# Filter MLP and FFN passage of a Hyena filter kernel: positions loaded in two halves, loads held back, and the first tile's sums put ahead of two units' spectra

## The chip, the cores and the metric

One core of one Trainium2 chip. Its engines are TensorE (PE: matrix products into PSUM), VectorE (DVE), ScalarE (ACT), GpSimd (POOL) and SyncE (SP, which only issues transfers). Each works through its own instructions in order; a semaphore holds an instruction until what it needs is done. Transfers (DMAs) are issued from the queues of SP, ACT and POOL and share 16 DMA engines. The metric is the device time of one execution in microseconds (us); lower is better.

## The reference

```python
h_filt = (np.maximum(pos_emb @ w1, 0.0) @ w2) * np.exp(-0.01 * np.arange(S))[:, None]
u = x * v                                   # x, v: (4, 12544, 128) float32
Uf = np.fft.rfft(u, n=2 * S, axis=1)
Hf = np.fft.rfft(h_filt, n=2 * S, axis=0)   # pos_emb: (12544, 64), w1: (64, 64), w2: (64, 128)
y = np.fft.irfft(Uf * Hf[None], n=2 * S, axis=1)[:, :S]
t = (x * y).reshape(50176, 128)
h = np.maximum(np.maximum(t @ moe_w1, t @ moe_w2), t @ moe_w3)   # 128 -> 768, moe weights float64
out = h @ moe_w_out                                              # 768 -> 128
```

A filter is made by a small MLP over position embeddings and damped by a window; the input is convolved with it along the sequence, gated by x, and sent through a maxout feed-forward network (FFN).

## The kernel before, in words

The long transform is split by hand into two steps: sums over 98 (or 82, for the filter) blocks of 128 positions give N1 = 90 values of an index k1, then a second step works per k1. Everything is float32. The schedule is manual: every engine executes in the order in which the Python code issues, and tile pools with a fixed number of buffers decide when a buffer may be written again.

1. **Prologue, to about 117 us.** PE runs products on a zero tile (`warm_up`, 4 records each). POOL issues the loads of the window, of an identity (`eye`), of a permutation (`back`) and of `w1`; SP and ACT issue eight loads of the position embeddings `pos` (64 rows at a time, 5.0 to 5.5 KB per row). `window_back` transposes the window on PE, lets ACT copy it into `winT`, multiplies by `back` and copies the result to `winr`. The filter MLP then has eight steps. `mlp_in(i)` is 32 matmuls (64 records and as many weight loads) into one of two PSUM tiles `pm`; it takes positions 127 - 16 i downward of each block, so steps 0 to 3 need columns 64 to 127 and steps 4 to 7 the rest. `mlp_out(i)` is two VectorE operations that apply ReLU and the window and write into `hs`. Between them VectorE multiplies the first two *units* of batch 0 (`u_mul`; a unit is 4 channels' worth of x and v, loaded by `u_load` in two DMAs of 196 KB with 392-byte pieces), and `turn2` transposes them on PE. Then come 16 *quads* of the filter (`quad`: 16 matmuls, one ACT copy) and 16 pairs of units, each two quads and a `turn2`. Beside them VectorE converts the FFN's float64 weights piece by piece (`some`, 12 operations for each of 8 jobs) from `raw` tiles; the first two raw loads are issued by SP in the prologue, the others by POOL.
2. **Second step of filter and batch 0, to about 303 us.** Per pair of k1: products, butterflies, the product with the filter's spectrum, and the way back; results go to DRAM (`zd`). At its end the first units of batch 1 are transposed for the next stage.
3. **Passage.** With the first FFN tile, `t_load` fetches the tile's z values (two DMAs) and x (four). `t_sums` forms sums and differences of the two z halves on VectorE, `t_last` multiplies them on PE by the inverse table `f4p` and VectorE multiplies the result by x into `gt`. Units 2 and 3 of batch 1 are treated here too: `u_products` does a unit's 16 matmuls (32 records) and an ACT copy `high` and returns a function that does its two VectorE operations (line 426), which write the *spectrum*; `u_first` is both at once.
4. **FFN with the convolutions of batches 1 to 3 beside it, to the end.** `up` makes a piece of the hidden layer (two products, an ACT ReLU and a VectorE maximum), `down` the product with `moe_w_out`; steps of the next batch's convolution are laid out by slot beside them (units 4 and 5 of batch 1 at slots 0 and 2). The last batch runs with fewer products.

Banks: `u_products` takes turns over two PSUM banks (`cps`), so unit 4 reuses the bank of unit 2 and unit 5 that of unit 3; `up` and the first `t_last` take turns over three (`hps`). Two buffers serve `high`, two serve `raw`.

Of the kernel before, what the change touches and what calls it, by code (L numbers as in the profile page):

```python
# [10 lines left out]
FP32 = mybir.dt.float32  # L11
# [5 lines left out]
P = 128  # L17
# [10 lines left out]
HH = NH // 2  # L28
# [63 lines left out]
def kernel(  # L92
# [15 lines left out]
    nc = tc.nc  # L108
    NG, _, _, B, NB = x.shape
    FO, S = posT.shape  # L110
# [18 lines left out]
    f1_d = nc.inline_tensor(f1_t, name="f1_const").ap()  # L129
    f1h_d = nc.inline_tensor(f1h_t, name="f1h_const").ap()  # L130
# [64 lines left out]
    def scratch(name, bufs):  # L195
        return sml.tile([P, 2 * HF], I32, tag=name, name=name, bufs=bufs)[:]

    def load_raw(i, h, eng):
        r = scratch("raw", 2)
        if i < 3:  # L200
            src = (moe_w1, moe_w2, moe_w3)[i].bitcast(I32).rearrange("(g c) f -> c g f", c=GC)
            for c in range(GC):
                eng.dma_start(r[c * NG:(c + 1) * NG],
                                  src[c][:, h * 2 * HF:(h + 1) * 2 * HF])
        else:
            src = moe_w_out.bitcast(I32).rearrange("(c p) d -> p c d", p=P)
            eng.dma_start(r.rearrange("p (c d) -> p c d", c=NF // 2),
                              src[:, h * NF // 2:(h + 1) * NF // 2, :])
        return r
# [52 lines left out]

    specH = pin.tile([P, N1, 2, FO], FP32, name="specH")
    pos = specH[:].rearrange("p k r f -> p (k r f)")[:, 0:HH * P]
    posv = pos.rearrange("f (n p) -> f p n", p=P)
    hs = spec[0:64 + HH].rearrange("p k r d -> p (k r d)")[:, 0:FO * P].rearrange(
        "n (f r t) -> n f r t", r=2, t=64)
# [2 lines left out]
    w2x = pin.tile([P, D], FP32, name="w2x")  # L270
    win = sml.tile([64 + HH, P], FP32, name="win")
    winT = sml.tile([P, 2, 64 + HH], FP32, name="winT")
    winr = sml.tile([64 + HH, 2, 64], FP32, name="winr")
    back = sml.tile([P, 2, 64], FP32, name="back")
    f1h = sml.tile([64 + HH, 2, 2 * N1], FP32, name="f1h")
    warm = sml.tile([P, 256], FP32, name="warm")
# [9 lines left out]
    nc.gpsimd.dma_start(eye[:], eye_d)  # L286
    nc.gpsimd.dma_start(back[:].rearrange("p r t -> p (r t)"), back_d)
    for h in range(2):
        nc.gpsimd.dma_start(w1_sb[64 * h:64 * h + 64], w1[:, :])
    cuts = (0, 11, 21, 31, HH)  # L290
    for j, (lo_, hi_) in enumerate(zip(cuts, cuts[1:])):
        for h in range(2):
            (nc.scalar if (h + j) % 2 else nc.sync).dma_start(
                pos[64 * h:64 * h + 64, lo_ * P:hi_ * P],
                posT[:, (h * HH + lo_) * P:(h * HH + hi_) * P])
    for r in range(2):
        nc.scalar.copy(winT[:, r, 0:64], warm[:, 0:64])

    def warm_up(n):

        ps = fps.tile([P, 1024], FP32, tag="cv", name="pw")
        for _ in range(n):
            halves_mm(ps[:, 0:256], warm[:, 0:P], warm[:], True, True)

    def window_back():
        pw = fps.tile([P, 1024], FP32, tag="cv", name="pw")
        nc.tensor.transpose(pw[:, 0:64 + HH], win[:], eye[0:64 + HH, 0:64 + HH])
        for r in range(2):
            for h in range(2):
                c = 64 * (h ^ r)  # L310
                nc.scalar.copy(winT[:, r, c:c + HH], pw[:, 64 * h:64 * h + HH])
        for r in range(2):
            nc.tensor.matmul(pw[0:64 + HH, 512 + 64 * r:576 + 64 * r], winT[:, r], back[:, r],
                             start=(r == 0), stop=True, skip_group_check=True)
        nc.scalar.copy(winr[:].rearrange("n r t -> n (r t)"), pw[0:64 + HH, 512:512 + P])

    def w2_order():
        nc.scalar.copy(w2x[:].rearrange("f (c g) -> f c g", c=GC),
                       w2_in[:].rearrange("f (g c) -> f c g", c=GC))

    def mlp_in(i):

        ps = pms[i % 2]
        for q in range(8):
            for r in range(2):
                for h in range(2):
                    c = 64 * (h ^ r)
                    nc.tensor.matmul(  # L328
                        ps[c:c + HH, 512 * r + q * FO:512 * r + (q + 1) * FO],
                        posv[64 * h:64 * h + 64, P - 1 - 2 * (8 * i + q) - r, :],  # L330
                        w1_sb[64 * h:64 * h + 64], start=(q == 0), stop=True,
                        skip_group_check=True)
    def mlp_out(i):
        v = pms[i % 2][0:64 + HH].rearrange("n (r t f) -> n r f t", r=2, t=8)
        for r in range(2):
            nc.vector.scalar_tensor_tensor(
                out=hs[:, :, r, 8 * i:8 * i + 8], in0=v[:, r], scalar=0.0,
                in1=winr[:, r, None, 8 * i:8 * i + 8].to_broadcast([64 + HH, FO, 8]),
                op0=ALU.max, op1=ALU.mult)
# [9 lines left out]
    def u_load(b, u):  # L349
        c, g0 = divmod(u, NG // 4)  # L350
        ts = []
        for src in (xr, vr):
            t = pools(b, u).tile([P, 4, NB], FP32, tag=f"u{len(ts)}", name="ut")
            nc.sync.dma_start(
                t[:], src[4 * g0:4 * g0 + 4, :, c, b, :].rearrange("g p n -> p g n"))
            ts.append(t)
        us[u] = ts

    def u_mul(u):
        a, v = us[u]  # L360
        nc.vector.tensor_tensor(out=a[:], in0=a[:], in1=v[:], op=ALU.mult)  # L361
# [68 lines left out]
    def u_first(*args):  # L430
        u_products(*args)()
# [269 lines left out]
    def t_sums(i, eng=nc.gpsimd, parts=(0, 1)):  # L701
        z0, z1 = zts[i]
        if 0 in parts:
            evens_[i] = hp.tile([N1, 512], FP32, tag="even", name="even", bufs=2)
        even = evens_[i]
        for a, (out, op) in enumerate(((even[:], ALU.add), (z1, ALU.subtract))):
            if a not in parts:
                continue
            if i[0] == 0 or i[1] < NT // 2:
                eng.tensor_tensor(out=out, in0=z0, in1=z1, op=op)  # L710
            else:
                nc.vector.scalar_tensor_tensor(out=out, in0=z1, scalar=sign_t[:, 0:1], in1=z0,
                                               op0=ALU.mult, op1=op)
        if 1 in parts:
            zts[i] = evens_.pop(i)[:], z1
# [145 lines left out]
    raws, todo = [], []  # L861
# [15 lines left out]
    def turn2(u):  # L877

        t = utp.tile([NB, 8, 2, 64], FP32, tag="uT", name="uT")
        ps = fps.tile([P, 1024], FP32, tag="cv", name="pst")  # L880
        for v in range(2):
            turn(u + v, ps[:, 512 * v:512 * v + 512])
        nc.scalar.copy(t[:], ps[0:NB, :].rearrange("n (s t r) -> n s r t", s=8, r=2))
        uts[u] = t
# [2 lines left out]
        ps = fps.tile([P, 1024], FP32, tag="cv", name="ps1")  # L887
        first_halves(ps, lhs, table, dst, nc.scalar.copy)

    warm_up(22)  # L890
    window_back()
    warm_up(3)
    nc.scalar.dma_start(f1h[:], f1h_d)
    nc.scalar.dma_start(w2_in[0:FO], w2[:, :])
    nc.scalar.dma_start(w2_in[FO:P], w2[:, :])
    nc.scalar.dma_start(f1q[:], f1_d)
    raws.append(load_raw(*jobs[0], nc.sync))
    u_load(0, 0)
    u_load(0, 1)
    raws.append(load_raw(*jobs[1], nc.sync))  # L900
    for u in range(2, 6):
        u_load(0, u)
    for i in range(9):
        if i < 8:
            mlp_in(i)
        if i:
            mlp_out(i - 1)
        if i in (4, 5):
            u_mul(i - 4)
        if i == 7:  # L910
            turn2(0)
    w2_order()
    mps.close()
    fps = fin.enter_context(tc.tile_pool(name="fps", bufs=4, space=PSUM))
# [217 lines left out]
    for n, (b, i) in enumerate(tiles[:LAST]):  # L1132
        if i == 0:
            plan, pairs_from = plans[b]
        if n == 0:
            t_load(*tiles[0])
            t_load(*tiles[1])
            u_first(2)
            third = u_products(3)
            t_sums(tiles[0], nc.vector)  # L1140
            t_last(tiles[0], next(hbanks))
            third()
        for f in range(NF):

            if i < NT - 2:
                if f == 0:
                    t_load(*tiles[n + 2])
            elif i == NT - 1 and f < 2 and n + 1 + f < len(tiles):
                t_load(*tiles[n + 1 + f])
            turn_ = i == NT - 1  # L1150
            if f == 4 and n + 1 == LAST:
                t_sums(tiles[n + 2], nc.vector)
            h = up((b, i), f)
            for a in range(2):
                if f == plan[i][a]:
                    t_sums(tiles[n + 1],
                           nc.vector if turn_ or i * NF > pairs_from else nc.gpsimd, (a,))
            late.append(((b, i), f, h))
            if len(late) > 2:
                down(*late.pop(0))  # L1160
            if f == plan[i][2]:
                t_last(tiles[n + 1])
            if f == 5 and n + 1 == LAST:
                t_last(tiles[n + 2])
            run(besides.pop(n * NF + f, ()))
# [28 lines left out]
    for i in range(0, NT, 2):  # L1194
        h = {}
# [67 lines left out]
```

## Time and profile before

| What | us |
|---|---|
| median of 3 runs | 2282.13 |
| lowest and highest | 2281.03, 2283.14 |
| profiled execution | 2286.24 |
| its span, first to last instruction | 2284.5 |
| PE busy | 2256.9 |
| DVE busy | 1561.3 |
| ACT busy | 1174.9 |
| POOL busy | 878.6 |

The profile is of one execution; positions in time are given from the start of its span. In its rows, "PE" is the matrix product and "PEld" the weight load that runs beside it; a row gives the line of the kernel, the engine, the operation, what it writes and reads, and behind an arrow what the engine last waited for. The chain of waits follows the work back from the last instruction to whatever released each step; "issue" in it is time in which the engine waited for nothing that the profile shows. Line 328 is `mlp_in`, 336 `mlp_out`, 165 a quad, 413 a unit's products in the later batches, 710 `t_sums`, 731 the product with x, and 156 a helper that all products in halves go through.

### The profile page before, as it was taken

The numbers are of one execution on the slowest core, as the hardware profiler recorded it, in microseconds if no ns is written. First come the engines' busy times: TensorE is split into PE (matmuls) and PEld (weight loads), VectorE is DVE, ScalarE is ACT, GpSimd is POOL, SyncE is SP. The second block draws the span as 40 slices with busy tenths as digits, with TensorE's granted clock in tenths as the row PEclk, the third lists the DMA queues.
The fourth block names the chain that finished last, engine by engine and source line by source line (L and its number), as shares of the span: only waits on it lengthen the run. The fifth ranks groups of instructions, "written<-read, shape, count | busy, mean of one in ns | idle before, by whom it ended". The sixth has DMA issues, their size and how long they took to land.

```text
span 2284.5 us, 68468 instructions
## 1 busy us (share of the span) xinstructions
PE 2256.9 (99%) x27855; PEld 1377.3 (60%) x27855; DVE 1561.3 (68%) x2854; ACT 1174.9 (51%) x2125; POOL 878.6 (38%) x1087
## 2 busy tenths in 40 slices
PE   8999999999999999999999999999999999999998
PEld 7989866655555556655555556655555556666665
DVE  5579867668787757657878756767878854544443
ACT  2688844456666534456666534456666622222222
POOL 2045434323333333423333334423333326666666
PEclk9999999999999999999999999999999999999999
DMA  8778989799999689879999889779999732222221
GB/s 182 188 220 278 303 178 182 141 217 245 238 220 245 181 171 174 164 186 250 238 234 239 206 162 186 160 174 254 234 241 238 199 86 56 56 68 64 62 56 22
DMA packets 473269, 411.03 MB, mean 180 GB/s; under 512 B 327865, under 2 KB 374426, under 8 KB 472954
## 3 DMA queue, kind: packets, MB, share of 16 engines
q1 hardware_dynamic: 445954, 329.48, 63.9%
q0 software_dynamic: 26288, 75.47, 11.0%
q8 instruction: 219, 3.59, 0.7%
q10 hardware_dynamic: 712, 1.70, 0.3%
q14 instruction: 96, 0.79, 0.1%
HBM read 262.84 MB, written 84.67 MB: 152 GB/s over the span
## 4 chain that ended last, share of the span: by engine, by line
PE 96%; DMA 1%; DVE 1%; issue 1%; ACT 0%; POOL 0%; SPq 0%; POOLq 0%; DVEq 0%; ACTq 0%
PE hps L156 44%; PE ops L156 19%; PE ops L804 6%; PE cps L413 5%; PE cps L156 4%; PE ps L156 3%; PE cps L474 3%; PE ps L165 3%; PE cps L484 3%; PE sps L1010 2%; PE gps L992 2%; PE last L156 1%; PE pst L366 1%; PE pm L328 1%; DMA back<-back_const 0%
## 5 line engine op out<-in xcount | busy, mean ns | idle before, releaser
L156 PE MATMUL hps<-gt,w_sb 128*64 128x392 f32 x6144 | 1150.7, 494 | 0.7 <-DVE gt L731 0.7
L741 ACT ACTIVATE hid<-hps 128x392 f32<-128x392 f32 x768 | 383.8, 500 | 703.3 <-PE hps L156 686.8
L156 PEld LDWEIGHTS hps<-gt,w_sb 128*64 128x64 f32 x6144 | 430.7, 137 | 422.0 <-issue 385.8
L744 DVE TENSOR_TENSOR hid<-hid,hps 128x392 f32<-128x392 f32 x768 | 428.3, 558 | 334.0 <-PE hps L156 325.6
L156 PE MATMUL ops<-hid,wo_sb 128*64 128x392 f32 x2304 | 480.0, 492 | 0.0
L526 POOL TENSOR_TENSOR cb<-cb,xs 128x512 f32<-128x512 f32 x135 | 174.1, 1290 | 462.6 <-DVE xs L523 345.8
L156 PEld LDWEIGHTS ops<-hid,wo_sb 128*64 128x64 f32 x2304 | 171.8, 137 | 207.4 <-issue 199.4
L426 DVE TENSOR_TENSOR spec<-cps,high 128x360 f32<-128x360 f32 x188 | 140.9, 790 | 127.2 <-ACT high L422 127.2
L499 DVE TENSOR_TENSOR cb<-cps,eo 128x512 f32<-128x512 f32 (+1 forms) x288 | 175.3, 650 | 74.0 <-ACT eo L496 74.0
L759 POOL DMA_DIRECT2D out_dram<-ot x96 | 75.4, 785 | 343.9 <-ACT ot L757 296.5
L514 ACT ACTIVATE xs<-cb 32x512 f32<-32x512 f32 x270 | 169.5, 628 | 20.5 <-DVE cb L499 11.5
L515 ACT COPY xs<-cb 32x512 f32<-32x512 f32 x270 | 166.3, 616 | 3.2
L422 ACT COPY high<-cps 128x360 f32<-128x360 f32 x94 | 75.0, 798 | 179.7 <-PE cps L413 145.9
L413 PEld LDWEIGHTS cps<-f1q,uT 98*64 98x64 f32 x3008 | 131.2, 138 | 29.3 <-issue 23.7
L530 DVE TENSOR_TENSOR xs<-cb 128x256 f32<-128x256 f32 x270 | 140.9, 567 | 9.2 <-POOL cb L526 9.0
L413 PE MATMUL cps<-f1q,uT 98*64 98x90 f32 x3008 | 135.5, 242 | 1.9 <-DVE uT L397 1.5
L382 POOL COPY planes<-ut 128x784 uint16<-128x784 uint16 x90 | 76.3, 848 | 155.0 <-DVE ut L361 141.3
L507 POOL DMA_DIRECT2D zd<-cb x135 | 92.8, 687 | 64.5 <-DVE cb L499 56.9
L156 PEld LDWEIGHTS cps<-f4p,even 90*64 90x64 f32 x1552 | 89.5, 138 | 35.0 <-issue 32.6
L828 POOL DMA_DIRECT2D out_dram<-o x128 | 77.7, 612 | 49.6 <-DVE o L821 47.9
L156 PE MATMUL cps<-f4p,zt 90*64 90x49 f32 x1552 | 96.3, 222 | 0.1
L156 PE MATMUL cps<-f4p,even 90*64 90x49 f32 x1552 | 95.0, 220 | 0.0
(143 smaller groups left out, 3149.4 us busy)
## 6 DMA issues: line engine op xcount, KB each, us to landing
ht<-hd SPq DMA_DIRECT2D x264, 256.0 KB, 6.7
wt<-wq_const SPq DMA_DIRECT2D x144, 256.0 KB, 6.2
zd<-cb POOLq DMA_DIRECT2D x135, 256.0 KB, 6.0
zt<-zd SPq DMA_DIRECT2D x384, 90.0 KB, 2.9
sq<-spec SPq DMA_DIRECT2D x264, 128.0 KB, 6.9
ut<-in_xr_dram SPq DMA_DIRECT2D x128, 196.0 KB, 4.1
ut<-in_vr_dram SPq DMA_DIRECT2D x128, 196.0 KB, 4.3
xT<-in_x_dram SPq DMA_DIRECT2D x256, 98.0 KB, 3.3
```

The lines of the kernel that those rows point to most:

```text
L156: nc.tensor.matmul(out[64 * h:64 * h + 64], lhsT[:, 64 * h:64 * h + 64], rhs, start=start, stop=stop, skip_group_check=True)
L413: nc.tensor.matmul(ps[64 * c:64 * c + 64, 256 * i + h * N1:256 * i + (h + 1) * N1], t[:, 2 * ((at + i) % 8) + h].rearrange("n r t -> n (r ...
L426: nc.vector.tensor_tensor(out=spec[:, :, a, at:at + n], in0=v[:, 1], in1=high, op=op)
L499: nc.vector.tensor_tensor(out=cb[:, a, lo:hi], in0=ps[:, lo:hi], in1=eo[:, lo:hi], op=op)
L507: nc.gpsimd.dma_start(zd[b][2 * z:2 * z + 2].rearrange("k c t a f -> (k c t) a f"), zss.pop(z))
L514: nc.scalar.mul(xs[at:at + 32], xt[at + 32:at + 64], -1.0)
L515: nc.scalar.copy(xs[at + 32:at + 64], xt[at:at + 32])
L526: nc.gpsimd.tensor_tensor(out=xts[g], in0=xts[g], in1=xs[:], op=ALU.add)
L530: nc.vector.tensor_tensor(out=ab[:, q], in0=y[:, 0], in1=y[:, 1], op=(ALU.subtract, ALU.add)[q])
L741: nc.scalar.activation(h[:], pa[:, 0:N], Relu)
L744: nc.vector.tensor_tensor(out=h[:], in0=h[:], in1=pb[:, 0:N], op=ALU.max)
L804: nc.tensor.matmul(ps[64 * c:64 * c + 64, 0:H2], w, rhs[:, H2 * c:H2 * c + H2], start=start, stop=True, skip_group_check=True)
```

## The change

- Loads of the positions: instead of eight loads of whole rows, two rounds of four. The first round takes columns 64 to 127 of every block of 128 positions, the second columns 0 to 63; each piece is 256 bytes. `w1` is issued ahead of them by SP and ACT instead of by POOL.
- Warm-up: 16 instead of 22 products in halves, and the 3 after the window are gone. The window's transpose moves behind the first MLP step, the product with `back` behind the second. `winr` is written twice, into the two `raw` buffers; the first serves outputs 0 to 4, the second 5 to 7.
- Order of loads: units 0 and 1 come right behind the positions. The filter's tables (`f1h`, `f1q`) and `w2` are issued by ACT after the window's copies, now in MLP step 1. The first raw weights are issued by SP at step 5, then units 2 to 5, and the second raw weights after the MLP.
- Passage: the products of units 2 and 3 are issued together, then VectorE takes the first tile's sums, then unit 2's spectrum, then the product with x; unit 3's spectrum follows behind the first `up`.

```diff
@@ -262,6 +262,7 @@
 
     specH = pin.tile([P, N1, 2, FO], FP32, name="specH")
     pos = specH[:].rearrange("p k r f -> p (k r f)")[:, 0:HH * P]
+    posn = pos.rearrange("f (n p) -> f n p", p=P)
     posv = pos.rearrange("f (n p) -> f p n", p=P)
     hs = spec[0:64 + HH].rearrange("p k r d -> p (k r d)")[:, 0:FO * P].rearrange(
         "n (f r t) -> n f r t", r=2, t=64)
@@ -270,7 +271,8 @@
     w2x = pin.tile([P, D], FP32, name="w2x")
     win = sml.tile([64 + HH, P], FP32, name="win")
     winT = sml.tile([P, 2, 64 + HH], FP32, name="winT")
-    winr = sml.tile([64 + HH, 2, 64], FP32, name="winr")
+    winrs = [scratch("raw", 2).bitcast(FP32)[0:64 + HH, 0:P].rearrange(
+        "n (r t) -> n r t", r=2) for _ in range(2)]
     back = sml.tile([P, 2, 64], FP32, name="back")
     f1h = sml.tile([64 + HH, 2, 2 * N1], FP32, name="f1h")
     warm = sml.tile([P, 256], FP32, name="warm")
@@ -286,13 +288,14 @@
     nc.gpsimd.dma_start(eye[:], eye_d)
     nc.gpsimd.dma_start(back[:].rearrange("p r t -> p (r t)"), back_d)
     for h in range(2):
-        nc.gpsimd.dma_start(w1_sb[64 * h:64 * h + 64], w1[:, :])
-    cuts = (0, 11, 21, 31, HH)
-    for j, (lo_, hi_) in enumerate(zip(cuts, cuts[1:])):
-        for h in range(2):
-            (nc.scalar if (h + j) % 2 else nc.sync).dma_start(
-                pos[64 * h:64 * h + 64, lo_ * P:hi_ * P],
-                posT[:, (h * HH + lo_) * P:(h * HH + hi_) * P])
+        (nc.scalar if h else nc.sync).dma_start(w1_sb[64 * h:64 * h + 64], w1[:, :])
+    for p0 in (64, 0):
+        for j, (lo_, hi_) in enumerate(((0, 21), (21, HH))):
+            for h in range(2):
+                (nc.scalar if (h + j) % 2 else nc.sync).dma_start(
+                    posn[64 * h:64 * h + 64, lo_:hi_, p0:p0 + 64],
+                    posT[:, (h * HH + lo_) * P:(h * HH + hi_) * P].rearrange(
+                        "f (n p) -> f n p", p=P)[:, :, p0:p0 + 64])
     for r in range(2):
         nc.scalar.copy(winT[:, r, 0:64], warm[:, 0:64])
 
@@ -302,17 +305,21 @@
         for _ in range(n):
             halves_mm(ps[:, 0:256], warm[:, 0:P], warm[:], True, True)
 
-    def window_back():
-        pw = fps.tile([P, 1024], FP32, tag="cv", name="pw")
+    pw = fps.tile([P, 1024], FP32, tag="cv", name="pw")
+
+    def window_turn():
         nc.tensor.transpose(pw[:, 0:64 + HH], win[:], eye[0:64 + HH, 0:64 + HH])
         for r in range(2):
             for h in range(2):
                 c = 64 * (h ^ r)
                 nc.scalar.copy(winT[:, r, c:c + HH], pw[:, 64 * h:64 * h + HH])
+
+    def window_back():
         for r in range(2):
             nc.tensor.matmul(pw[0:64 + HH, 512 + 64 * r:576 + 64 * r], winT[:, r], back[:, r],
                              start=(r == 0), stop=True, skip_group_check=True)
-        nc.scalar.copy(winr[:].rearrange("n r t -> n (r t)"), pw[0:64 + HH, 512:512 + P])
+        for winr in winrs:
+            nc.scalar.copy(winr.rearrange("n r t -> n (r t)"), pw[0:64 + HH, 512:512 + P])
 
     def w2_order():
         nc.scalar.copy(w2x[:].rearrange("f (c g) -> f c g", c=GC),
@@ -332,6 +339,7 @@
                         skip_group_check=True)
     def mlp_out(i):
         v = pms[i % 2][0:64 + HH].rearrange("n (r t f) -> n r f t", r=2, t=8)
+        winr = winrs[i > 4]
         for r in range(2):
             nc.vector.scalar_tensor_tensor(
                 out=hs[:, :, r, 8 * i:8 * i + 8], in0=v[:, r], scalar=0.0,
@@ -887,28 +895,31 @@
         ps = fps.tile([P, 1024], FP32, tag="cv", name="ps1")
         first_halves(ps, lhs, table, dst, nc.scalar.copy)
 
-    warm_up(22)
-    window_back()
-    warm_up(3)
-    nc.scalar.dma_start(f1h[:], f1h_d)
-    nc.scalar.dma_start(w2_in[0:FO], w2[:, :])
-    nc.scalar.dma_start(w2_in[FO:P], w2[:, :])
-    nc.scalar.dma_start(f1q[:], f1_d)
-    raws.append(load_raw(*jobs[0], nc.sync))
-    u_load(0, 0)
-    u_load(0, 1)
-    raws.append(load_raw(*jobs[1], nc.sync))
-    for u in range(2, 6):
+    warm_up(16)
+    for u in range(2):
         u_load(0, u)
     for i in range(9):
         if i < 8:
             mlp_in(i)
+        if i == 0:
+            window_turn()
+        if i == 1:
+            window_back()
+            nc.scalar.dma_start(f1h[:], f1h_d)
+            nc.scalar.dma_start(w2_in[0:FO], w2[:, :])
+            nc.scalar.dma_start(w2_in[FO:P], w2[:, :])
+            nc.scalar.dma_start(f1q[:], f1_d)
         if i:
             mlp_out(i - 1)
         if i in (4, 5):
             u_mul(i - 4)
+        if i == 5:
+            raws.append(load_raw(*jobs[0], nc.sync))
+            for u in range(2, 6):
+                u_load(0, u)
         if i == 7:
             turn2(0)
+    raws.append(load_raw(*jobs[1], nc.sync))
     w2_order()
     mps.close()
     fps = fin.enter_context(tc.tile_pool(name="fps", bufs=4, space=PSUM))
@@ -1135,11 +1146,10 @@
         if n == 0:
             t_load(*tiles[0])
             t_load(*tiles[1])
-            u_first(2)
-            third = u_products(3)
+            second_, third = u_products(2), u_products(3)
             t_sums(tiles[0], nc.vector)
+            second_()
             t_last(tiles[0], next(hbanks))
-            third()
         for f in range(NF):
 
             if i < NT - 2:
@@ -1151,6 +1161,8 @@
             if f == 4 and n + 1 == LAST:
                 t_sums(tiles[n + 2], nc.vector)
             h = up((b, i), f)
+            if n == f == 0:
+                third()
             for a in range(2):
                 if f == plan[i][a]:
                     t_sums(tiles[n + 1],
```

## The prediction

> **What bounds the kernel now.** I read the page's busy line and its chain first, then the chain of waits over 0 to 40 us and over 255 to 330 us, then the windows, DMA and tile views there.
>
> ```profile
> span 2284.5 us, 68468 instructions
> PE 2256.9 (99%) x27855; PEld 1377.3 (60%) x27855; DVE 1561.3 (68%) x2854; ACT 1174.9 (51%) x2125; POOL 878.6 (38%) x1087
> PE 96%; DMA 1%; DVE 1%; issue 1%; ACT 0%; POOL 0%; SPq 0%; POOLq 0%; DVEq 0%; ACTq 0%
> ```
>
> PE holds 96% of the chain: time can be won only where PE idles or runs slowly, and a microsecond won there ahead of the FFN should move everything after it. The chain over 0 to 40 us (start, length, what):
>
> ```profile
> 3.40 10.66 DMA back<-back_const
> ...
> 16.19 2.90 PE pm L328 x98
> 19.09 1.86 issue
> 20.95 3.73 PE pm L328 x120
> 24.68 1.65 issue
> 26.33 3.45 PE pm L328 x119
> 29.78 1.65 issue
> 31.43 4.04 PE pm L328 x119
> ...
> 36.51 1.02 ACT uT L883
> ...
> 37.58 2.46 PE ps L165 x57
> ```
>
> The filter MLP starts at 16.2 us, because PE first runs warm-up products, waits for `eye` and `back` (back lands at 14.06) and runs 3 more warm-ups. It then runs for 19.3 us with three gaps ("issue": nothing shown is waited for), and the first spectrum quad starts at 37.58. The passage to the FFN, from the chain over 255 to 330 us:
>
> ```profile
> 304.59 0.81 ACT high L422
> ...
> 306.11 0.76 DVE spec L426
> 306.87 0.61 DVE even L710
> 307.50 0.70 DVE zt L710
> ...
> 310.63 2.88 PE hps L156 x8
> ```
>
> VectorE does unit 2's spectrum (L426) first and the first tile's sums (L710) second; PE waits for the sums. And the windows view (length, busy time by engine, granted clock, DMA share):
>
> ```profile
> 308.30:315.10 6.80, 6.14 (x61) 4.32 (x62) 2.50 (x4) 0.50 (x1) 2.77 (x3) 0.50 0.46 105
> ```
>
> After that idle time PE runs at half clock for 6.8 us.
>
> [...] The gaps stand 256 instructions apart (128 matmuls and 128 weight loads, as the windows view counts for 20.9 to 24.7 us), so I take them for that refill, but 1.65 to 1.86 us is not hidden. [...]
>
> **Positions in halves.** Before, 2.69 MB in rows of 5.0 to 5.5 KB at 235 GB/s (3 to 14 us), all needed before the first MLP step. Now 256-byte pieces, half of them first: 41 x 128 = 5248 pieces, 1.34 MB, enough for steps 0 to 3; the rest serves steps 4 to 7. No 256-byte plain load is in the trace. The nearest rows are the 392-byte unit loads:
>
> ```profile
> q1 hardware_dynamic: 11550, 4.39, 95.8%
> ```
>
> That is 80 to 100 us: 0.958 x 16 x 20 us / 11550 = 26.5 ns of an engine each. [...] Bounds: 17.3 ns (by bytes alone) and 26.5 ns (as much as a 392-byte one). With 328 pieces per engine a half takes 5.7, **6.3** or 8.7 us. The first data moved near 2 us; with w1 now ahead of it on the same two queues and POOL's 0.15 MB between, the first half lands at 2.2 + 6.3 + 0.7 = 9.2 us (8.6 to 11.6), the second near 15.8 (15 to 21). Two more DMA issues (w1 moves from POOL to SP and ACT) at about 0.6 us each delay those queues, neither of which computes then.
>
> **Warm-ups.** 22 become 16: 6 x 4 records x 108 ns (74 records in 8.00 us, windows view of 4.5 to 12.5) = 2.6 us off a stretch that ended at 12.5, so PE is free at 9.9 us. The 3 after the window, 1.45 us, go.
>
> **The MLP.** A step is 64 matmul records: 2.97 us / 114 x 64 = 1.67 us. Step 0 runs 9.9 to 11.6. The window's transpose now sits behind step 0; everything after it on PE waits for `eye`, 12.7 at worst[...]. ACT's 4 copies take 1 us beside step 1 (ends 13.6 to 14.5), then the window products (0.55), a copy (0.3; the second copy runs beside the next step), and VectorE's first output from 14.6 to 15.9 (1.29). Step 2 follows at 16.0: the copies and the wait bring back 2.4 us of idle time[...]. Then PE sets the pace, VectorE needing 1.3 per step: six steps x 1.67 + two refills x 1.7 = 13.4, so step 7 ends at 29.4; transposes 1.05 and the copy 1.06 lead to the first quad at 31.6. Gain 37.58 - 31.6 = 6.0; with `eye` at 12.7 and a third refill exposed 3.2. I take **5.5**, range 2 to 7.
>
> **What is held back.** The first raw weights (SP) now wait for output 4 (about 23 to 24 us), because `winr` lives in their buffer; units 2 to 5 are queued behind them on SP: 0.39 + 1.57 MB at 242 GB/s = 8 us, so done by 33. Unit 2 is wanted 3.5 us of conversions after the MLP (before: 36.7 to 40.2), near 34; the second raw waits for the last output (31), lands near 35 and is wanted near 36.5. I cost this at nothing: the cover is the DMA queue that was empty before (7 GB/s in 31.4 to 35.4 us) and 12 conversions of 0.35 to 0.56 us. Without that cover each microsecond late stalls VectorE and after it the second pair's transposes.
>
> **From the first quad to the passage** the same instructions run in the same order, PE bound (2.63 of 3.64 us per pair in quads, the rest transposes); waits on DMAs at 263 and 287 us are relative to issues that shift too. I pass the gain on whole, give or take 1.5 us for refills that fall elsewhere.
>
> **The passage.** The first tile's two z loads are issued at 300.6 and 301.7 and land 3.7 us later (tile view), by 305.4. The sums can run 305.4 to 306.8 in the place of the spectrum, PE's products in 0.92 us at full clock (32 records at 322.6) until 307.9; the spectrum (1.44) delays the product with x to 308.3 (x itself lands near 307.4), and the up product starts at 308.9 instead of 310.63: 1.7 us. `third` goes behind the first maximum; unit 5's products, its next taker, came 6 us after unit 4's, and that covers it. The clock: 310.63 to 315.12 at half clock is 2.25 us of lost work. Idle time falls to 2.1 us in three pieces[...]. I take **3.0**, range 0.5 to 4.
>
> **Sum**: 5.5 + 3.0 = 8.5 us. The profiled execution took 2286.24 (span 2284.5 and 1.7 around it), 4.1 above the median of 2282.13; an execution like it would take 2277.7, and the median becomes 2273.6.
>
> **Rivals.** *Half of it only* (0.22): the window's constants or the second half of the positions come late, or the held loads do, so the MLP gives 1 to 2 us, with 3 from the passage: 4 to 5, so 2277.5. For it: `eye` took 9.9 us. Against: its delay came with the positions' queues, which are not longer now. *The passage gives nothing* (0.13): the clock drops as before and x is late; 5.5, so 2276.6. [...] Against: the sums themselves bound PE. *Slower* (0.07): 256-byte pieces are far dearer. The first quad follows the second half's landing by four steps, two refills and 2.1 us, 12.2 in all; the gain is gone at a landing of 25.4, with the passage at 28.4, and 4.6 us slower needs 33.0: (33.0 - 2.2) / 656 = 47 ns a piece, 1.8 times what a 392-byte one costs. Then some 2288. *It doesn't do what it says*: the loads are not truly held back, since SP's queue already waited for position loads (6.5 us in its waits); that leaves the gain of the halves as it is.
>
> **How the numbers follow.** Both parts work: 0.58, with 2273.6 and its own range of 2270 to 2277. A measurement here can tell about 0.2%, 4.6 us: 2277.5 is the border. Faster: 0.56 of the first case, 0.11 of the half case, 0.10 of the next = 0.77; same: the rest of these, 0.16; slower 0.07. The range is 2269.5 to 2280: from both best ends to the half case with its later refills.
>
> **What would show it.** The first L328 row near 10 us in place of 16.2, the first quad near 32, fewer "issue" pieces in the MLP; the sums ahead of the spectrum and the up product about 1.7 us closer to unit 3's products; a shorter stretch at 0.50. I am wrong if steps 4 to 7 wait for the positions, if the conversions wait for the raw weights, or if the spectra after 60 us start to wait for loads.

## The result: 0.18% slower, where a gain of 8.5 us was forecast

| | before | after |
|---|---|---|
| median, 21 runs each | 2282.13 | 2287.22 |
| lowest to highest | 2280.23 to 2284.92 | 2280.53 to 2290.70 |
| profiled execution | 2286.24 | 2288.12 |
| its span | 2284.5 | 2286.3 |

The ratio is 1.0018, with an interval of 1.0013 to 1.0024: about 4 us slower (5.1 by the medians), and the runs of after scatter more. The page of after, span, busy line and chain shares:

```profile
span 2286.3 us, 68401 instructions
PE 2256.2 (99%) x27819; PEld 1375.7 (60%) x27819; DVE 1561.1 (68%) x2854; ACT 1174.8 (51%) x2126; POOL 876.3 (38%) x1085
PE 96%; DMA 2%; DVE 1%; issue 0%; ACT 0%; POOL 0%; SPq 0%; POOLq 0%; DVEq 0%; ACTq 0%
```

PE still bounds the kernel, so what follows is again a matter of PE's waits. Line numbers have moved: `mlp_in` is now L335, `mlp_out` 344, `t_sums` 718, the product with x 739, `u_mul` 369, `turn2`'s transposes 374, its copy 891, `raw` loads 203 and their conversion 224 to 241. The chain of waits over 0 to 75 us:

```profile
2.26 10.08 DMA specH<-in_pos_emb_dram
...
18.29 0.79 PE pm L335 x23
19.08 3.20 issue
22.28 3.73 PE pm L335 x127
...
35.29 8.90 PE ps L165 x224
...
52.48 8.33 DMA raw<-in_moe_w_dram
...
60.94 0.36 DVE ta L224
...
63.69 0.49 DVE ut L369
...
64.31 1.95 PE pst L374 x8
66.25 3.44 PE ps L165 x64
```

There are two stories here. Up to 35 us the MLP starts early, with two records at 11.01, then waits for the rest of the first half of the positions and runs on from 12.48. PE's timeline (start, length, engine, line; in brackets the idle time before it and what ended it):

```profile
11.01 0.33 PE L335 MATMUL pm<-w_sb,specH 64*41 64x64 f32 x2
12.48 1.70 PE L335 MATMUL pm<-w_sb,specH 64*41 64x64 f32 x62 [1.15 <-DMA specH<-in_pos_emb_dram]
```

In step 2 it stands still for 3.20 us after 23 records; the first quad comes at 35.29, 2.3 us earlier than in the first profile of before. The gaps of before in the MLP stood 256 of PE's instructions apart (128 products and 128 weight loads from 20.95 to 24.68), and so does this one from the next (127 and 127 recorded from 22.28 to 26.01); such places are called block boundaries below. A packet of instructions (queue q8) moved near these gaps: in before from 18.40, 23.52 and 29.06, for 1.18, 1.30 and 0.98 us, with PE at work again 1.4 to 1.5 us after it ended; in after from 19.28 for 1.54 us, with PE at work again 1.5 us after its end. Then, at 61 us, the chain has left PE: it runs through a load of raw FFN weights (8.33 us), through VectorE's conversion of them, and through `u_mul` (L369, the product x times v of unit 4) before PE may transpose unit 4 at 64.31. VectorE's and SP's timelines of after tell where that began:

```profile
29.58 1.73 SPq L203 DMA_DIRECT2D raw<-in_moe_w_dram  x4
...
36.85 2.67 SPq L203 DMA_DIRECT2D raw<-in_moe_w_dram  x4
...
47.72 0.36 DVE L224 TENSOR_SCALAR ta<-raw 128x384 int32<-128x384 int32 x1 [7.49 <-DMA raw<-in_moe_w_dram]
...
64.31 1.95 PE L374 MATMUL pst<-eye,ut 128*98 128x128 f32 x8 [4.97 <-DVE ut L369]
```

The last row of these is PE's. The second raw tile is issued at 36.85, behind units 2 to 5, and lands near 47.6. Two buffers serve `raw`, so the fourth raw load can be issued only when the second tile has been read: its last reader (L235) ends at 50.47, POOL issues at 51.02 (the profile names a unit load, landed at 50.78, as the last thing that POOL waited for), the load takes 8.33 us, and the fourth conversion starts at 60.94. `u_mul` of unit 4 stands behind eight of its operations in VectorE's order. In before none of this shows: SP issued the second raw load at 18.5, and no conversion waited before 60.0.

The windows of after (from:to, length, busy time of PE, PEld, DVE, ACT and POOL with counts, granted clock, DMA share, GB/s):

```profile
2.00:20.00 18.00, 14.15 (x219) 9.74 (x215) 3.92 (x6) 2.59 (x9) 1.95 (x4) 1.00 1.24 170
20.10:30.30 10.20, 7.27 (x255) 6.97 (x255) 5.13 (x9) 0.00 (x0) 0.00 (x0) 0.50 0.49 100
...
36.85:47.60 10.75, 10.75 (x254) 10.30 (x252) 3.32 (x8) 7.08 (x9) 2.00 (x4) 1.00 1.08 216
...
61.10:67.90 6.80, 3.59 (x32) 3.03 (x34) 6.59 (x18) 1.01 (x1) 1.99 (x4) 0.50 0.33 97
310.20:317.10 6.90, 6.24 (x66) 4.41 (x64) 3.67 (x6) 0.50 (x1) 2.76 (x3) 0.51 0.55 139
```

And the queues of ACT (q10) and SP (q1) in 2 to 12 us (packets, MB, time of the packets as a share of 16 engines' time):

```profile
q10 hardware_dynamic: 3557, 0.90, 58.9%
q1 hardware_dynamic: 2736, 0.69, 44.9%
```

The third row of the windows is the time between the issue of the second raw tile and its landing. Both stalls go with half clock: the granted clock was 0.50 for 10.2 us from inside the gap in the MLP on, and for 6.8 us around the wait at 61, where the first pair's quads take 3.44 us in place of 2.63. The last window is the passage, whose stretch at half clock is as long as in before. Its chain in after:

```profile
300.91 2.88 DMA zd<-zs
...
303.81 0.98 SPq L687
...
304.84 3.58 DMA zt<-zd
...
308.54 0.70 DVE even L718
...
310.00 1.58 PE hps L156 x28
...
312.23 2.88 PE hps L156 x8
```

The sums now wait for the z load itself, and it for the last store of the stage before. That store lands 0.9 us ahead of the linear layer's copy (`lin`, 304.73), and the z load goes out then; in before it was issued 2.0 us ahead of `lin`.

### The profile page after: what moved, and what is told of

Same layout as the page of the kernel before. It is cut to its first block, busy times and chain, and to the rows that moved or that the text cites. A ratio compares the mean times of both kernels' runs of the same rounds, so it can differ in the third digit from the quotient of the medians.

```text
span 2286.3 us, 68401 instructions
## 1 busy us (share of the span) xinstructions
PE 2256.2 (99%) x27819; PEld 1375.7 (60%) x27819; DVE 1561.1 (68%) x2854; ACT 1174.8 (51%) x2126; POOL 876.3 (38%) x1085
## 4 chain that ended last, share of the span: by engine, by line
PE 96%; DMA 2%; DVE 1%; issue 0%; ACT 0%; POOL 0%; SPq 0%; POOLq 0%; DVEq 0%; ACTq 0%
PE hps L156 44%; PE ops L156 19%; PE ops L812 6%; PE cps L421 5%; PE cps L156 4%; PE ps L156 4%; PE cps L482 3%; PE cps L492 3%; PE ps L165 2%; PE sps L1021 2%; PE gps L1003 2%; PE last L156 1%; PE pst L374 1%; PE pm L335 1%; DMA specH<-in_pos_emb_dram 0%
## 5 line engine op out<-in xcount | busy, mean ns | idle before, releaser
L522 ACT ACTIVATE xs<-cb 32x512 f32<-32x512 f32 x270 | 169.6, 628 | 20.5 <-DVE cb L507 11.6
```

Source lines behind the costliest of these rows:

```text
L522: nc.scalar.mul(xs[at:at + 32], xt[at + 32:at + 64], -1.0)
```

## The experiments

The positions in time of each profile, in us from its start; "up" is the start of the first up product.

| kernel | first quad | last quads of the units | `lin` | up | span | ratio to before |
|---|---|---|---|---|---|---|
| before | 37.58 | 111.35 | 302.65 | 310.63 | 2284.5 | |
| before_again | 36.33 | 109.77 | 300.08 | 308.08 | 2281.4 | |
| after | 35.29 | 114.34 | 304.73 | 312.23 | 2286.3 | 1.0018 [1.0013, 1.0024] |
| after_again | 35.26 | 115.50 | 306.84 | 314.44 | 2288.7 | |
| e1_passage | 36.03 | 109.47 | 300.44 | 306.64 | 2280.3 | 0.9999 [0.9990, 1.0007] |
| e2_prologue | 35.16 | 114.44 | 305.01 | 312.85 | 2288.3 | 1.0011 [1.0002, 1.0020] |
| e3_raw_first | 34.96 | 110.93 | 301.81 | 309.35 | 2283.6 | 1.0005 [0.9997, 1.0014] |
| e4_whole_rows | 35.88 | 111.45 | 301.63 | 309.03 | 2284.9 | 1.0013 [1.0005, 1.0022] |
| e5_early_z | 36.09 | 110.94 | 301.27 | 306.22 | 2277.6 | 0.9983 [0.9975, 0.9992] |
| e6_not_held | 34.96 | 108.14 | 298.59 | 306.42 | 2280.0 | 1.0001 [0.9993, 1.0010] |
| e7_long_free | 35.79 | 109.23 | 299.35 | 306.98 | 2281.5 | 0.9993 [0.9985, 1.0001] |
| e8_long_raw_first | 31.31 | 107.80 | 299.05 | 307.01 | 2280.3 | 0.9988 [0.9981, 0.9994] |
| e9_split_z | 31.73 | 106.31 | 296.91 | 306.63 | 2280.6 | 1.0001 [0.9993, 1.0010] |
| e10_mul_first | 34.96 | 111.23 | 302.17 | 309.29 | 2283.7 | 1.0010 [1.0002, 1.0018] |

From "up" to the end of the span takes 1973.3 to 1975.9 us in all of them but e5 (1971.4): what is won or lost ahead of the FFN is passed on nearly whole.

**Which half of the change loses?** e1 is before with the new passage, e2 is after with the old one.

```diff
@@ e1_passage, against before (e2_prologue is the reverse, against after) @@
-            u_first(2)
-            third = u_products(3)
+            second_, third = u_products(2), u_products(3)
...
+            second_()
...
-            third()
...
+            if n == f == 0:
+                third()
```

> The kernel before with the new passage alone. Theory L (the second raw weights come late in the prologue and hold VectorE, the passage is a small gain): 0.5 to 1.5 us faster than before, since the first tile's z values land only about when VectorE was free anyway. The prediction's own step said 3.0 us faster. Rival P (the passage is what costs): slower than before by 3 us or more.

> The changed kernel with the old passage. Theory L: 5 to 7 us slower than before, a little more than the changed kernel, with VectorE waiting some 7 us for the second raw weights and PE some 5 us for unit 4. Rival P: within 1 us of before or faster.

Measured: e1 0.9999, e2 1.0011. The prologue loses and the passage gains nothing that 13 runs can tell, although e1's profile has the up product 6.2 us after `lin` in place of 8.0. The chain of e1 goes over the x load, which is issued behind z; below it is VectorE's timeline:

```profile
298.38 0.99 SPq L679
...
301.91 3.33 DMA xT<-in_x_dram
...
303.22 0.69 DVE L710 TENSOR_TENSOR even<-zt 90x512 f32<-90x512 f32 x1 [5.47 <-DMA zt<-zd]
303.94 0.69 DVE L710 TENSOR_TENSOR zt<-zt 90x512 f32<-90x512 f32 x1
304.63 1.48 DVE L426 TENSOR_TENSOR spec<-cps,high 128x360 f32<-128x360 f32 x2
306.02 0.56 DVE L731 TENSOR_TENSOR gt<-hps,xT 128x392 f32<-128x392 f32 x1
```

x has landed by 305.3, but VectorE works without a break from the landing of z on: the sums from 303.22, then the spectrum, then the product with x at 306.02. e2 has the waits of after to within 0.4 us: 7.23 and 3.61 for raw weights, 5.06 of PE for `u_mul`. Its loss, 0.11%, is about 2.5 us, half of the 5 to 7 expected.

**Is it the late second raw load?** e3 issues it right behind the first, ahead of units 2 to 5. Outputs 0 to 4 of the MLP take turns over the two `raw` buffers for `winr`, and 5 to 7 use a tile of their own.

```diff
+    winrs.append(sml.tile([64 + HH, 2, 64], FP32, name="winr")[:])
...
-        winr = winrs[i > 4]
+        winr = winrs[2 if i > 4 else i % 2]
...
             raws.append(load_raw(*jobs[0], nc.sync))
+            raws.append(load_raw(*jobs[1], nc.sync))
             for u in range(2, 6):
                 u_load(0, u)
...
-    raws.append(load_raw(*jobs[1], nc.sync))
```

> The changed kernel with the second raw weights issued right behind the first, ahead of units 2 to 5 (outputs 5 to 7 read the window from a tile of their own, so that neither load waits longer than output 4). Theory L: the 7 us wait of VectorE and the 5 us wait of PE go, the stretch at half clock near 61 us with them; 3 to 6 us faster than before, so 8 us or more faster than the changed kernel. Rival B (the 256-byte pieces cost it): stays slower than before, since the first spectrum quad already starts earlier than before and the loss would have to sit elsewhere.

Measured: the raw wait is 0.94 us, PE's wait for unit 4 is gone, the last quads come at 110.93 in place of 114.34, and the ratio falls from 1.0018 to 1.0005; the intervals overlap only at 1.0013 to 1.0014. The 3 to 6 us ahead of before that were expected did not come: with the stall gone the kernel is level with before, not faster.

**Is it the wait for raw weights, or the product queued behind it?** e10 leaves the raw loads where after has them and issues `u_mul` of units 4 and 5 on VectorE ahead of those conversions.

```diff
             if u and k in (0, 1):
                 u_mul(2 * u + k)
+                u_mul(4 + k)
...
-            if u + 4 < NU:
+            if u and u + 4 < NU:
                 u_mul(u + 4 + v)
```

> Edit on the kernel after: the DVE product u_mul of unit 4 is issued ahead of the conversion of the second raw weight tile instead of behind the queue that waits for raw weights. Theory of the late raw weights (their lateness reaches PE only through the DVE products queued behind the waiting conversions): the conversion still waits about 7 us for the raw tile, but PE's wait of 4.97 us for unit 4 at 64.31 shrinks to under 2 us, the last quads of the units come 3 to 4 us earlier (near 111), time 2283 to 2285 against 2287.2. Rival (PE needs the converted weights themselves as well, or the lateness moves to the unit behind): last quads stay at 114, time as after, 2286 to 2288.

The chain of e10 runs on PE without a step from 44 to 59 us but for one gap at a block boundary, and on from there:

```profile
44.87 11.81 PE ps L165 x293
56.69 2.06 issue
58.75 4.19 PE ps L165 x59
```

The second conversion starts at 46.71, only 1.0 us earlier than in after; it waits 1.94 us itself, because VectorE spends the rest of the wait on the products ahead of it and on their data, and a later conversion still waits 3.12 us for its raw tile. But PE's wait for unit 4 is gone and the last quads come 3.1 us earlier, at 111.23. So the late weights reach PE through the product that is queued behind them. The time, 2285.45, lies 0.5 above what this theory expected; its interval overlaps that of after, and e2, which has the stall, has nearly the same ratio. So e10 shows the path in the trace, not its price in time.

**Is the stall one execution's accident?**

> The kernel after once more, for a second profile. Theory of the late raw weights: the wait of about 7 us of the second conversion (47.7) and PE's wait of 4 to 5 us for unit 4 are there again, last quads 113.5 to 114.5. Rival (they belong to one execution): the second conversion waits under 3 us, last quads near 110.

> The kernel before once more, for a second profile. Theory of the clock[...]: the first quad falls anywhere from 36.0 to 37.6, the MLP's gaps at block boundaries between 0.5 and 1.9 us each, no wait of DVE for raw weights over 1 us, last quads 109.5 to 111.4. Rival (the profile shown is what each execution does): first quad 37.6 and last quads 111.35 again to 0.3 us.

Measured: after_again has it too, 7.90 us for the second conversion and 4.17 us of PE, with the last quads at 115.50. before_again has no raw wait over 1 us (VectorE idles 2.61 us ahead of a conversion at 59.36, about where before waits 2.00), its gaps at block boundaries are 0.51, 1.36 and 0.27 us where the first profile had 1.65 to 1.86, and its first quad is at 36.33. The profile that the prediction started from had a slow MLP.

**Nothing held back.** e6 issues raw weights and units 2 to 5 in the prologue again, with tiles of its own for `winr`; the 256-byte halves stay.

```diff
-    winrs = [scratch("raw", 2).bitcast(FP32)[0:64 + HH, 0:P].rearrange(
-        "n (r t) -> n r t", r=2) for _ in range(2)]
+    winrs = [sml.tile([64 + HH, 2, 64], FP32, name=f"winr{_}")[:] for _ in range(2)]
...
+    raws.append(load_raw(*jobs[0], nc.sync))
...
+    raws.append(load_raw(*jobs[1], nc.sync))
+    for u in range(2, 6):
+        u_load(0, u)
...
-            raws.append(load_raw(*jobs[0], nc.sync))
-            for u in range(2, 6):
-                u_load(0, u)
...
-    raws.append(load_raw(*jobs[1], nc.sync))
```

> The changed kernel with nothing held back: the window's copies have tiles of their own, and raw weights and units 0 to 5 are issued ahead of the MLP in the order of before; the positions stay in 256-byte halves. Theory L: no wait of VectorE for the second raw weights, first quad near 35.5 us, 1 to 4 us faster than before. Rival B (the halves cost it): the refills and the second half come later with more traffic, the first quad is at 37 us or later, and it is not faster than before.

Measured: last quads at 108.14, ratio 1.0001, with an interval that ends at 1.0010 where that of after begins at 1.0013. The loss, about 3.9 us, is gone: the holding back caused it. The 1 to 4 us ahead of before that were expected did not come either: without it the 256-byte halves bring no gain that these runs can tell.

**What do the pieces cost?** e4 is after with the old loads of whole rows. e7 is e6 with the halves laid out one behind the other in DRAM, so that a piece has 5.0 to 5.3 KB.

```diff
@@ e4_whole_rows, against after @@
-    for p0 in (64, 0):
...
+    cuts = (0, 11, 21, 31, HH)
...
@@ e7_long_free, against e6 @@
-                    posn[64 * h:64 * h + 64, lo_:hi_, p0:p0 + 64],
...
+                    pos2[64 * h:64 * h + 64, p_, lo_ * 64:hi_ * 64],
+                    posT[:, h, p_, lo_ * 64:hi_ * 64])
```

> The changed kernel with the positions loaded in whole rows again (eight loads), all else as changed. Theory L: the MLP starts near 15 us, the second raw weights are as late as before, so VectorE and PE still wait: slower than before by 3 to 8 us. Rival B: at the time of before or faster[...].

> The same with the positions laid out on the host so that a half is one run of 5.0 to 5.3 KB per row (no arithmetic; the position tile is laid out likewise). If the 256-byte pieces delay the MLP (the first half landed at 12.3 us, 10496 pieces at about 30 ns of an engine each), the first half lands near 9 us, the MLP starts near 10.7 and the first quad is near 33; 2 to 4 us faster than with 256-byte pieces. If pieces don't matter: within 1 us of it.

Measured: e4's MLP runs from 16.25, 3.8 us after that of after (12.48), and its first quad comes only 0.6 us later: with whole rows, landed by 16.16, the boundary inside step 2 costs no gap (279 records follow each other from 23.30; one gap of 0.25 us is left in the MLP). Its raw waits are 5.30 and 3.50 us, but PE waits only 0.2 us for unit 4, behind a gap of 2.06 us at a block boundary, and its last quads come at 111.45; its ratio, 1.0013, can't be told from that of after. e7 against e6 is 0.9993 against 1.0001, with intervals that overlap. Its first half landed at 12.11, not near 9, and its first quad was no earlier (35.79): part of the stretch up to there ran at half clock (the granted clock was 0.93 in 2 to 20 us, and the eight transposes at 32.74 took 1.95 us, as those of after did at 0.50).

**Long halves, held back, second raw load first.** e8 joins e7's loads with e3's order.

> Long halves with the loads held back, the second raw weights right behind the first (as in the run with the raw weights first). Theory L with the cost of the pieces: first quad near 31 to 32 us, no wait for raw weights above 1 us; 3 to 6 us faster than before, the best so far. Rival H (what starts earlier waits later for the loads that were held): the first quad gains but units or raw weights come late, and the last filter and unit quads end no earlier than in the run with the raw weights first (111 us).

The chain of e8:

```profile
31.31 8.90 PE ps L165 x224
...
52.76 2.56 issue
55.32 4.20 PE ps L165 x59
```

Measured: 2279.84 over 21 runs, 0.9988 [0.9981, 0.9994]. It beats both kernels: of those that compute the reference it is the only one whose interval lies below 1. By the ratio it is 2.7 us faster than before, just short of the 3 to 6 expected. From e3 it differs in the layout of the positions alone, and their intervals do not overlap (e3: 0.9997 to 1.0014): next to held loads the 256-byte pieces cost about 0.17%. The first quad comes at 31.31, near the prediction's 31.6, with two gaps of 0.65 and 0.35 in the MLP. Of the 5.0 us by which that leads before_again, 2.0 are left at the last quads. Between the two, one gap grew from 0.92 to 2.56 us, and the granted clock in 35 to 60 us was 0.93 in place of 1.00, which is some 3.5 us of half clock; the 59 records behind the gap take 4.20 us, where 64 took 2.70. Part of that is this one execution: in e9, whose prologue is the same, 3.5 of 4.6 us are left.

**What can the passage give?** In e5 (e1's order) the first tile's z is read from a buffer that was filled long before, in place of the convolution's result, so its first tile is not the reference's; the loads keep their size. e9 is e8 with the first tile's z load split: the first 42 pairs of k1, then x, then the last three pairs.

```diff
@@ e5_early_z, against e1 @@
+            if b == 0 and i == 0:
+                nc.sync.dma_start(zt[NK * c:NK * c + NK], hd[:, 2 * c:2 * c + 2, :])
+                continue
@@ e9_split_z, against e8 @@
+            if b == i == 0:
+                z_part(c, 0, NK - 3)
+                late_z.append((c, NK - 3, NK))
+                continue
...
+        for part in late_z:
+            z_part(*part)
```

> The kernel before with the new passage, and the first FFN tile's z values read from the filter's spectra in DRAM, written long before, in place of batch 0's result (so the first tile's output is another): its loads no longer wait for the last store of batch 0. Theory Z (the passage gained little because the z loads, issued when the last store has landed, set the time of the sums): z and x are issued about 2 us earlier, the sums start as soon as VectorE is free, and the first up product comes 1.5 to 2.5 us earlier against the copy to lin (6.2 us after it in the passage alone, 8.0 before): 1 to 3 us faster than the passage alone. Rival C (PE's clock decides the passage, not the loads): no difference beyond 1 us.

> Edit on the last kernel (long halves, held back, second raw weight first): the first tile's z load is cut by pairs of k1. Rows 0 to 41 of each half are read as soon as the store of their pairs has landed, x follows, and only the last three pairs' rows wait for the last store. Passage theory (the gain of the reorder is bounded by the landing of the last store and the whole z load behind it): the even sums start about 2 us earlier after lin's end, first up product about 5 to 6 us after the linear layer's end instead of 7.96, time 2277 to 2278.5 against 2279.84. Rival (small last load takes as long as the whole one[...], or the clock decides): no change, 2279 to 2280.5.

Measured: e5's up product starts 4.95 us after `lin`, PE runs on without half clock (the eight records of the first up product take 1.54 us, 2.88 in e1), and the ratio is 0.9983 against e1's 0.9999. This is what an early z would be worth: 2.7 us by the spans, 3.7 by the ratios, whose intervals touch. e9 missed: up comes 9.7 us after `lin` and the ratio is 1.0001. SP's timeline of e9 shows why:

```profile
295.66 1.82 SPq L688 DMA_DIRECT2D zt<-zd  x2
297.53 2.01 SPq L715 DMA_DIRECT2D xT<-in_x_dram  x4
299.58 1.49 SPq L688 DMA_DIRECT2D zt<-zd  x2
```

I had put the last three pairs behind x, whose issues hold SP for 2.0 us. They go out 2.7 us after `lin` (296.91), and the sums start at 302.76. A split with them ahead of x was not tried.

## Why the prediction was wrong, step by step

- **What is held back: the step that gave the wrong sign.** It was costed at nothing, with the second raw tile landed near 35. It landed near 47.6, 12.6 us later, for three reasons. The MLP ran late: the first raw load was issued at 29.58 instead of 23 to 24, and the last output, which the second raw load has to wait for, ended at 34.53 instead of 31. Then eight unit loads held SP from 31.4 to 36.7, so that the second raw load was issued at 36.85. And it took 10.8 us to land instead of 4, behind those loads and beside others: the DMA engines were 1.08 busy. The cover that I named, an empty DMA queue, was thus missing both as order on SP's queue and as bandwidth. The price of losing it was stated there (VectorE stalls, then the second pair's transposes), and it came: 4.97 us of PE and about 1.75 us through half clock in the first pair (3.44 for 2.63, and transposes in 1.95 for 1.01). In the traces e6, e3 and e10 take this loss away in three ways; in time only e6's interval is clear of that of after.
- **From the first quad to the passage.** The gain was to be passed on whole, give or take 1.5 us. From first quad to last quads before took 73.8 and 73.4 us in its two profiles, after 79.1 and 80.2. Even with the raw load first it is 76.0 (e3), 76.5 (e8) and 74.6 (e9), against 73.2 with nothing held (e6): the loads that were held now run there. In e8 the DMA engines are 0.96 busy in 35 to 60 us, 0.74 in before_again, and the block boundary costs 2.56 in place of 0.92 (1.24 in e9). That this comes from those loads fits, but was not shown apart: the one packet of instructions that moved there took about 1.2 us in both.
- **The MLP: 2.3 us in place of 5.5**, and 1.0 against before_again. Of the 3.7 us by which the first quad missed 31.6, step 2's start at 18.29 for 16.0 makes 2.3; it goes back to the landing of the first half of the positions. The gaps, refills in the prediction, make 0.6 (3.20, 0.75 and 0.03 for two of 1.7), and the rest fits the half clock, which the working left out (127 products took 3.73 us in after at 0.50; 128 took 3.45 in before at 1.00, from 26.33). The gap inside step 2 was to cost nothing, since PE's wait for `winr` lies just ahead of it; that was my estimate, and no trace had shown it. In after the wait ended at 18.29, PE ran through 23 records, and 3.20 us passed before the next, more than any of the three gaps of before (1.65 to 1.86). That e8's first quad, 31.31, meets the forecast of 31.6 is partly luck: its step 2 began 1.6 us late, at 17.62, and its gaps of 0.65 and 0.35 were 2.4 us shorter than forecast.
- **Positions in halves.** The first half landed at 12.35 for 9.2, past my bound of 11.6. The working gave that half the DMA engines to itself, and it did not have them. In 2 to 12 us of after, ACT's queue had moved 0.90 MB, of which its part of the first half is 0.67, when SP's queue was only finishing its own part: the second half moved beside the first. With pieces of 5 KB the first half landed hardly earlier, at 12.11 (e7), 11.68 (e8) and 12.18 (e9), so the price of a piece alone does not explain it. Of the 6.3 us for a half only the bounds came from the trace of before (5.7 and 8.7 us, from 17.3 and 26.5 ns a piece); the value between them was my choice and is not confirmed: in 2 to 20 us of after, two queues moved 5799 + 5392 packets, most of them these pieces, in (62.8 + 54.8)% of 16 engines' time. That is 30 ns each, but shares that add up to more than 1 count some time twice; by the count alone an engine had at most 16 x 18 us / 11191 = 25.7 ns for each, hardly less than the 26.5 of a 392-byte piece. The window's 170 GB/s compare with 226 in before_again.
- **The passage: 0.5 us closer in the profile for 3.0 forecast, and nothing that the runs can tell.** The mechanism was right (sums ahead of the spectrum; up starts 7.5 us after `lin` for 8.0 in the profiles of after and before), its size was not. I took z to land by 305.4, 2.8 us after `lin`, because it had done so in before. In e1, with the old prologue, the sums did start 2.8 us after `lin`, and up came 1.8 us closer, for 1.7 forecast. In after they waited for z until 308.54, 3.8 us after `lin`, behind the last store. The z load goes out 1.7 to 2.1 us ahead of `lin` in the three profiles with the old prologue that read the true z (before, before_again, e1), and 0.6 to 1.3 us ahead in the ten with a new one; why that is so is not shown. PE ran at half clock in after as in before (0.51 in 310.2 to 317.1 us, 0.50 in 308.3 to 315.1), so the 2.25 us that the prediction counts as lost to it were not won back.
- **The slower rival** was right in sign and wrong in cause: it needed 47 ns a piece and a late first quad, and the first quad came early. The chance of 0.07 for all that is slower was too small because the one step costed at nothing had only its sizes checked, not its order.

What stays open: why the runs of after scatter over 10 us. Its five runs with a mean granted clock of 0.994 average 2288.7 us and the three with 0.997 average 2281.5; a stall and the half clock behind it come together, and which comes first is not told by these runs.

## What to carry to other kernels

A load that is held back is also moved behind everything that its queue issues in between, so follow the order on the queue to the landing, then to the reader, and then to the first instruction behind that reader that the bounding engine needs (in after: second raw load issued at 36.85, landed near 47.6, first read at 47.72, PE waiting until 64.31 for `u_mul` behind a later conversion). With two buffers a late load also delays the one after the next (here the fourth: the last reader of the second tile ends at 50.47, the issue follows at 51.02). And check a step costed at nothing with two profiles: before's own first quad lay 1.25 us apart in two executions, half of what after's profile seemed to gain.

## What was not expected of the hardware

- PE's gap at the block boundary in step 2 was longer with small pieces: 2.07 to 3.20 us in the six profiles with 256-byte pieces. It was 0.65 to 0.82 us in the three with long ones (e7, e8, e9), and e4, with whole rows, had none there.
- A wait of PE just ahead of a block boundary did not spare the gap there: in after PE waited 1.68 us for `winr`, until 18.29, ran 23 records, and stood still from 19.08 for 3.20 us. The only packet of instructions in 16 to 24 us moved from 19.28 on. That this packet was PE's is inferred from its time.
- The half clock falls elsewhere from run to run: one profile of before has 6.8 us at 0.50 in the MLP (21.57 to 24.99 and 31.81 to 35.23), the other has 1.00 in 20 to 35 us and 0.91 in 0 to 20 us, which is some 3.6 us of half clock; there the three warm-ups ahead of the MLP took 2.72 us, 1.52 in the first profile.
